# A new order table for a delta-rule attention followed by a SoLU block

## The chip, the cores and the metric

The kernel runs on one core of a Trainium2 chip. A core has five engines that run side by side, each with its own queue of instructions, executed in the order in which they were put there: PE (TensorE, matrix products; its weight loads are counted apart as PEld), DVE (VectorE), ACT (ScalarE), POOL (GpSimd) and SP (SyncE, which here only issues transfers). Transfers (DMA) between the chip's memory and the core's on-chip memory are issued by SP or ACT and run on 16 DMA engines. Products land in PSUM, a small memory of banks, from which DVE and ACT fetch them. The metric is device time in microseconds (us) of one execution; less is better.

## What is computed

```python
# q, k, v: (4, 8, 768, 48) f32; beta: (4, 8, 768)
k_n = k / (norm(k, axis=-1) + 1e-06)
state = zeros((B, H, D, D))
for t in range(S):
    y[:, :, t] = einsum('bhd,bhde->bhe', q[:, :, t], state)
    v_old = einsum('bhde,bhd->bhe', state, k_n[:, :, t])
    state = state + beta_t * einsum('bhd,bhe->bhde', k_n[:, :, t], v_t - v_old)
x = y.transpose(0, 2, 1, 3).reshape(3072, 384)

h = x @ w_in                      # (384, 1024)
sm = softmax(h)                   # with the row's maximum taken off
solu = h * sm
ln = (solu - mean(solu)) / sqrt(var(solu) + 1e-06) * g_ln
out = ln @ w_out                  # (1024, 384)
```

The first part is a recurrence over 768 time steps for 32 pairs of batch and head; the second works on 3072 rows, each by itself. The weights w_in and w_out come as 64-bit numbers.

## The kernel before

**Tiling.** The 768 steps are cut into 12 chunks of 64. Two chunks make a stage, so there are 6 stages (s = 0 to 5). The batches go in two pairs. A *unit* n (0 to 23) is one chunk of one pair of batches with 8 heads each: 128 rows of x. Four units make a stage: n = 4s to 4s + 3. Unit n + 2 continues the state of unit n.

**A stage.** Within a chunk the recurrence becomes a triangular system per head. For each unit `gram_p` (words p and g of the order table) multiplies keys by queries and keys by keys (L444, L447); the first result is masked into `pt` (`p_mask` on DVE, L459, or `p_copy` on ACT with `p_pool` on POOL, L462 and L465), the second is copied by `g_copy` (L471). `g_out` (go, L481) writes it to memory, and `to_inv` (ti, L490) and `to_gx` (tg, L500) read it back in the layout of the inverse. `norms` (no, L512 to L520) makes the keys' norms on DVE. Then `inv_bm`, `inv_ya` (L579, on POOL), `inv_yb` (L586) and `inv` (in, L596 and L600) invert 128 triangular blocks of 32 x 32 a stage, by 30 steps of a product and a sum, each step needing the one before; a word such as `in.4.7.9.1` holds steps 7 and 8 of stage 4, and its last digit chooses POOL (1) or DVE (0). `inv_tz` and `inv_tx` (L606, L613) transpose the result, and the `tlevel` functions (ta, tm, tb, tc; L687 to L711) complete it to 64 x 64. Stage 0 has Gram products of its own (gd, gl), a transpose `gram_dt` (gt), an inverse of blocks of 16 (iv) and levels la, lm, lb, lz, lc, lx above it.

**The state's chain.** For each unit, in turn: `chain_bank` (bk, L730), `chain_r` (r, L736, DVE), `chain_ups` (up, L750), `chain_u` (u, ACT), `chain_kpu` (kp, L774 and L776), `chain_s` (s, L783).

**The MoE part of a unit.** x is split into a high and a low float16 half (y and xl; L788, L792) and transposed by a transfer (xT, L796). `moe_h` (h, L808) makes h in three passes `h.n.0` to `h.n.2` of six products: high by high, high by low, low by high. `sm_max`, `sm_exp`, `sm_pr` (mx, ex, pr), `sm_square` (sq), `sm_z`, `sm_var`, `sm_rr` (z, va, rr), `sm_ln`, `p_hi`, `p_lo` (ln, ph, pl) make the normalized rows, a transfer transposes them (pT, L866), and `moe_o` (o, L873) multiplies by w_out in three passes of eight products. `moe_out` and `store` (ou, st) write out.

**Weights.** `load_w` (W) brings one of 14 blocks: 0 to 5 of w_in (L204), 6 to 13 of w_out (L207). Their 64-bit words are turned into float32 by `w_abs` on ACT and `w_bits` (wb): pieces 0, 1, 2 on DVE (L266, L268, L270) and a last one that is piece 3 on DVE or piece 4 on POOL (L276, L277). Then the high half is made on ACT (wh), the low half on DVE (wl) or on PE and ACT (wu, wc).

**Other loads.** Kn and V bring keys and values of a stage, `L` the key and query block of a unit, LK and LA only its keys (LA by ACT's queue), LQ only its queries; B and G are small.

**Fillers.** fy, fh and fm (`fill`, L188) are products of the identity into a PSUM tile that nobody reads: `fh.7` issues seven.

**The order.** Nothing is scheduled by the compiler: a text, ORDER, holds some 1250 words; each word calls one function with its arguments, and each engine's queue gets its instructions in the order of the words. Waits for data and for buffers follow from the tiles. So a word that stands early holds up whatever stands behind it on the same engine, and SP's transfers also go out in the order of the words. A transfer can be issued by ACT in place of SP where the word ends in 1 (go, ti, tg).

Of the kernel before, what the change touches and what calls it, by code (L numbers as in the profile page):

```python
# [31 lines left out]
V.0.0 W.1 wb.8.1 wb.3.0 wb.10.1 wb.3.1 wl.4 wb.3.2 wb.5.1 lc.1 ta.0 tm.0 lz.1 lc.0 wb.1.0 wb.8.2 lx.0.0 wb.10.2 wa.1
tb.0 tc.0 fv.0.0.1 wb.9.4 wh.9 z1 wb.10.3 wb.1.1 wb.5.2 wb.1.2 wb.1.3 wl.9 p.0 pa.0 pm.0 wb.3.4 wh.3 wh.10 lx.1.1
ti.1.0 up.0 wb.5.4 wb.8.4 gr.1 wh.1 no.1 bm.1 u.0 LQ.1 W.2 wh.5 fh.1 LQ.3 V.1.0 fh.7 ta.1 p.1 kp.0 pa.1 pm.1 wu.5 tm.1
tb.1 wa.2 wc.5 s.0 y.0 la.3 wu.1 W.11 tc.1 wc.1 ya.1 fv.1.0.1 yb.1 in.1.1.3.1 in.1.3.5.1 in.1.5.7.1 in.1.7.9.1
# [1 line left out]
in.1.27.29.1 in.1.29.31.1 wu.3 up.1 lm.3 xl.0 W.0 L.8 LQ.2 lb.3 W.7 xT.0 fy.5 wa.0 wa.11 wb.2.0 wb.2.1 wb.2.2 wl.10
wb.2.3 wb.11.0 wb.0.0 wb.0.1 wb.0.2 wb.0.3 u.1 lz.3 p.8 kp.1 wc.3 wh.2 g.8 wh.0 s.1 pa.8 la.2 h.0.0 wl.2 lm.2 lb.2
wl.0 h.0.1 lc.2 wb.11.1 y.1 pm.8 xl.1 wa.7 lz.2 ta.2 lx.2.1 wh.8 tm.2 W.6 wa.6 h.0.2 tb.2 V.0.1 wb.6.0 wb.6.1 wb.6.2
wb.7.0 wb.7.1 wb.7.2 wb.7.3 wh.7 L.11 L.9 L.10 tc.2 bk.2 gl.0.3 mx.0 wb.11.2 wb.11.3 r.2 ex.0 pr.0 p.10 pa.10 wl.7  # L40
pm.10 up.2 Kn.0.1 xT.1 g.10 V.1.1 p.2 pa.2 wh.11 u.2 sq.0 pm.2 wl.8 wb.6.3 wl.11 W.13 W.12 go.0.2.0 h.1.0 p.9 pa.9
pm.9 kp.2 wh.6 g.9 p.11 h.1.1 h.1.2 wa.13 g.11 y.2 gc.0.3 ta.3 tm.3 lc.3 lx.3.1 tb.3 tc.3 wb.13.0 wb.12.0 wb.12.1 s.2
z.0 xl.2 wb.13.1 wb.12.2 wl.6 mx.1 bk.3 wb.13.2 r.3 va.0 ex.1 wa.12 pr.1 rr.0 wb.13.4 fm.6 up.3 u.3 p.3 pa.3 pm.3 kp.3
sq.1 tz.1 ln.0 pc.11 y.3 zc.1.0 tx.1.0 s.3 xl.3 zc.1.1 tg.1.0 go.1.2.0 fv.0.1.1 z.1.1 pp.11 L.14 xT.2 h.2.0 h.2.1
h.2.2 ta.4 xo.1.0.1 tm.4 mx.2 bk.4 xo.1.1.0 tb.4 r.4 fm.3 ta.5 ex.2 pr.2 ti.2.0 L.13 V.1.2 xT.3 tc.4 tm.5 up.4 ta.6
tb.5 va.1.1 wb.12.4 z.2.1 wh.12 sq.2 fv.1.1.1 fh.7 u.4 tc.5 tm.6 wh.13 ph.0 kp.4 h.3.0 tb.6 ta.7 y.4 h.3.1 tm.7 tc.6
# [922 lines left out]
```

## Time and profile before

| | us |
|---|---|
| median of 3 runs | 414.24 |
| lowest, highest run | 411.41, 414.56 |
| the profiled execution | 411.82 |
| its span, first to last instruction | 410.1 |
| DVE, ACT, POOL busy in it | 285.4, 238.7, 227.6 |

The profile comes from one execution. Its span leaves out 1.7 us at the ends. Busy time is the time in which an engine worked on an instruction; PE's products are pipelined, and the ends that the profile gives them are modelled. The granted clock is what the chip's throttle gave PE, 1.00 being full speed. A wait is put down to the instruction or transfer that ended it; "issue" is time in which an engine waited for nothing that the profile shows.

### The profile page before, as it was taken

Reading aid. Unit: us, or ns where it says so; the run is one execution under the profiler, and the core shown is the slowest. Engines: PE = TensorE matmul, PEld = TensorE weight load, DVE = VectorE, ACT = ScalarE, POOL = GpSimd, SP = SyncE. Lnnn points to the kernel's source line nnn. Section 1 sums busy time; section 2 is a strip of 40 time slices with the busy share of each in tenths; the row PEclk is TensorE's granted clock in tenths of the full one; section 3 lists DMA queues with packets and bytes.
Section 4 is the critical chain, followed back from the end, with each engine's and each line's share of the span. In section 5 each row is a group of like instructions: output and inputs, shape, how many; then the busy total and the mean of one; then the engine's idle time right before and its main releaser. Section 6 shows DMA issues by size and latency. Waiting matters only on the chain.

```text
span 410.1 us, 19489 instructions
## 1 busy us (share of the span) xinstructions
PE 359.0 (88%) x8697; PEld 228.0 (56%) x8697; DVE 285.4 (70%) x539; ACT 238.7 (58%) x486; POOL 227.6 (55%) x393
## 2 busy tenths in 40 slices
...
PEclk9755698968998699959999999999999999999999
...
GB/s 211 270 144 207 247 105 237 154 78 164 110 173 152 72 144 138 233 78 94 175 201 139 164 163 140 176 111 151 104 109 114 107 49 134 84 91 91 121 97 104
DMA packets 114645, 57.82 MB, mean 141 GB/s; under 512 B 102529, under 2 KB 105729, under 8 KB 114561
## 3 DMA queue, kind: packets, MB, share of 16 engines
...
q8 instruction: 68, 1.11, 1.2%
...
q14 instruction: 17, 0.13, 0.1%
...
## 4 chain that ended last, share of the span: by engine, by line
PE 68%; DVE 9%; POOL 7%; issue 6%; DMA 6%; ACT 4%; SPq 1%; POOLq 0%; DVEq 0%; ACTq 0%
PE h L808 22%; PE ops L873 19%; PE bank L730 4%; PE p L444 4%; PE kpu L774 4%; DMA kq<-kq_dram 2%; PE ups L750 2%; PE mps L703 2%; DMA wo<-w_out_dram 2%; PE yps L776 2%; PE mps L687 2%; PE yps L730 1%; PE fill L188 1%; PE g L447 1%; POOL itmp L596 1%
## 5 line engine op out<-in xcount | busy, mean ns | idle before, releaser
L596 POOL TENSOR_TENSOR itmp<-y,ginv 128x30 f32<-128x30 f32 (+14 forms) x116 | 65.3, 563 | 32.8 <-DVE y L600 14.8
L808 PE MATMUL h<-win_hi,xt 128*128 128x512 f16 x288 | 73.7, 392 | 5.5 <-issue 3.1
L873 PEld LDWEIGHTS <-ph 128*128 128x128 f16 x576 | 54.5, 99 | 41.0 <-DMA ph<-pn 4.1
L873 PE MATMUL ops<-wout_hi,ph 128*128 128x384 f16 x384 | 71.1, 331 | 3.3 <-ACT o L877 2.2
L600 POOL TENSOR_TENSOR y<-y,itmp 128x30 f32<-128x30 f32 (+14 forms) x116 | 66.1, 570 | 9.1
L808 PEld LDWEIGHTS <-xt 128*128 128x128 f16 x432 | 40.4, 100 | 53.1 <-issue 12.1
L444 PE MATMUL p<-kq 48*64 48x64 f32 x768 | 34.8, 250 | 9.7 <-DMA wo<-w_out_dram 5.4
L817 DVE TENSOR_REDUCE st<-h 128x1 f32<-128x1024 f32 x24 | 29.2, 1218 | 15.9 <-PE h L808 13.6
L444 PEld LDWEIGHTS p<-kq 48*64 48x64 f32 x768 | 31.1, 162 | 13.5 <-issue 8.1
L808 PE MATMUL h<-win_lo,xt 128*128 128x512 f16 x144 | 37.1, 396 | 0.3 <-issue 0.3
L873 PE MATMUL ops<-wout_lo,ph 128*128 128x384 f16 x192 | 36.5, 335 | 0.0
L828 DVE SCALAR_TENSOR_TENSOR pr<-h,pr 128x1024 f32<-128x1024 f32 x24 | 29.3, 1220 | 9.8 <-ACT pr L823 9.6
L862 DVE TENSOR_TENSOR pn<-pr,pn 128x1024 f16<-128x1024 f32 x24 | 30.5, 1276 | 7.0 <-ACT pn L858 7.0
L855 ACT ACTIVATE pr<-pr,st 128x1024 f32<-128x1024 f32 x24 | 29.8, 1241 | 7.7 <-POOL st L851 7.4
L823 ACT ACTIVATE pr<-h,st 128x1024 f32<-128x1024 f32 x24 | 26.7, 1112 | 12.0 <-DVE st L818 11.8
L850 POOL TENSOR_TENSOR st<-st,nhalf 128x1 f32<-128x1 f32 x24 | 14.0, 583 | 33.6 <-DVE st L846 18.5
L711 ACT COPY zt<-mps 32x128 f32<-32x128 f32 x96 | 24.5, 255 | 11.1 <-PE mps L703 9.8
L730 PE MATMUL yps<-st,kq 48*64 48x48 f32 x704 | 27.0, 226 | 3.6 <-issue 3.6
L836 ACT ACTIVATE pn<-pr,st 128x1024 f32<-128x1024 f32 x24 | 27.5, 1147 | 3.5 <-DVE st L829 3.3
L776 PE MATMUL yps<-u,pt 64*64 64x48 f32 x768 | 28.5, 224 | 1.0 <-DVE pt L459 0.7
L447 PE MATMUL g<-kq 48*64 48x64 f32 x640 | 27.4, 245 | 1.1 <-ACT u L757 1.0
L755 ACT ACTIVATE u<-ups 128x192 f32<-128x192 f32 x24 | 7.9, 329 | 34.5 <-PE upo L750 33.9
...
## 6 DMA issues: line engine op xcount, KB each, us to landing
...
gd<-g SPq DMA_DIRECT2D x8, 512.0 KB, 3.3
...
wi<-w_in_dram SPq DMA_DIRECT2D x6, 512.0 KB, 6.8
...
```

What stands on the lines that cost most here:

```text
L444: nc.tensor.matmul(out=ps[o : o + C, h], lhsT=k[lan, 0, h], rhs=k[lan, 1, h], start=True, stop=True)
L447: nc.tensor.matmul(out=gp[o : o + C, h], lhsT=k[lan, 0, h], rhs=k[lan, 0, h], start=True, stop=True)
L596: eng.tensor_tensor(out=tv, in0=y[:, 0:j, j : j + 1].to_broadcast([P, j, n]), in1=b[:, j : j + 1, j + 1 : 32].to_broadcast([P, j, n]), op= ...
L600: eng.tensor_tensor(out=y[:, 0:j, j + 1 : 32], in0=y[:, 0:j, j + 1 : 32], in1=tv, op=ALU.add)
L730: nc.tensor.matmul(out=ps[o : o + C, h], lhsT=k[lan, i, h], rhs=sb[lan, h], start=i == 0 or h == 0, stop=i == 0)
L776: nc.tensor.matmul(out=yps[n][o : o + C, h], lhsT=p[lan, h], rhs=u[lan, h], start=n < 2, stop=n < 2 or h == H - 1)
L808: nc.tensor.matmul(out=hp[n][:, qs], lhsT=xt[n][:, 3 * a + k], rhs=b[:, k, qs], start=j == 0 and k == 0, stop=j == 2 and k == 2,)
L817: nc.vector.tensor_reduce(out=nmax, in_=hp[n], op=ALU.max, axis=AX.X, negate=True)
L828: nc.vector.scalar_tensor_tensor(out=pr, in0=hp[n], scalar=1.0, in1=pr, op0=ALU.mult, op1=ALU.mult, accum_out=sp)
L855: nc.scalar.activation(pro[n], pro[n], AF.Identity, bias=mean, scale=rr)
L862: nc.vector.tensor_tensor(out=pn[:, 1], in0=pro[n], in1=pn[:, 0], op=ALU.subtract)
L873: nc.tensor.matmul(out=ops_[n], lhsT=pht[n][:, 8 * a + k], rhs=b[:, k], start=j == 0 and k == 0, stop=j == 2 and k == 7)
```

## The change

Only ORDER is replaced; no function is touched. The new table has 1246 words where the old one had 1257. All words of the fillers are gone. Most other words are the same and stand in another order; some change their last digit, so that a step runs on another engine or a transfer goes out by another queue:

- weights: the last piece is done by DVE in place of POOL for blocks 3, 4, 8, 9, 12 and 13, by POOL in place of DVE for blocks 0, 1 and 10; the low half of block 4 is made on PE and ACT, that of block 1 on DVE, each the other way round from before
- masks of units 4, 6 and 11: DVE in place of ACT and POOL
- inverse: 14 words `in` on DVE where there were 17, and others than before; steps 9 and 10 of stage 0 on POOL
- transfers of the Gram blocks: go.1.1 and go.0.3 by SP in place of ACT; tg.1, tg.5 and go.0.4 by ACT in place of SP
- small steps z, va, xo, lx and fv of some units and stages change engines

The diff cut to the first lines, those around the first w_out product and the last ones:

```diff
-Kn.1.0 kx.1.0 kv.1 Kn.0.0 G kx.0.0 kv.0 ca cn fy.13 fh.12 LA.0 LA.1 gd.0.0 gd.0.1 LK.2 gd.0.2 gz.0 z0 cc cb LK.3 B L.4
-fy.6 kr.0 kn.0 kb.0 iz.0 iy.0 gd.0.3 gt.0 ib.0 iv.0.1.3.0 iv.0.3.5.0 iv.0.5.7.0 iv.0.7.9.0 W.8 iv.0.9.11.0 p.4 gg.0
-pc.4 g.4 pp.4 L.5 W.4 W.9 L.7 L.6 W.10 W.3 W.5 p.5 wb.9.0 pc.5 g.5 pp.5 gl.0.0 gl.0.1 p.7 iv.0.11.13.1 iv.0.13.15.1
-pa.7 pm.7 wa.8 g.7 gc.0.0 wa.10 go.1.1.1 p.6 g.6 sg wb.4.0 wb.4.1 wb.4.2 wb.10.0 tz.0 wb.9.1 gl.0.2 pc.6 pp.6 wa.9
...
+W.4 wb.4.0 wb.4.1 Kn.1.0 kx.1.0 kv.1 cc ca iz.0 z1 z0 LA.0 Kn.0.0 LA.1 cn gl.0.0 kx.0.0 kv.0 W.5 wb.5.0 wb.5.1 wb.5.2
+wa.5 kr.0 LK.2 B LK.3 gd.0.0 gd.0.1 gd.0.2 gd.0.3 cb gz.0 wb.5.4 wa.4 gc.0.0 L.5 gl.0.1 p.5 kn.0 kb.0 iy.0 gt.0 W.1 G
+W.10 LQ.0 ib.0 iv.0.1.3.0 iv.0.3.5.0 iv.0.5.7.0 wb.1.0 iv.0.7.9.0 W.0 L.4 L.6 L.7 gl.0.2 gc.0.2 pc.5 g.5 wb.4.2 wb.4.3
+wb.0.0 wb.0.1 pp.5 iv.0.9.11.1 iv.0.11.13.1 iv.0.13.15.1 wh.5 gg.0 wa.10 wa.1 gc.0.1 p.4 pa.4 pm.4 wb.1.1 wb.1.2
+wb.0.2 g.4 wu.5 wh.4 p.7 pa.7 pm.7 V.1.0 W.2 g.7 wa.0 p.6 L.9 W.9 V.0.0 wu.4 tz.0 pa.6 pm.6 tx.0.0 wb.1.4 g.6 la.0
...
+pa.3 pm.3 tz.1 ta.3 lc.3 tm.3 sq.1 go.1.2.0 go.0.2.0 xT.2 W.8 ti.2.0 lx.3.1 tb.3 tc.3 up.3 tx.1.0 u.3 xo.1.0.1 p.13
+kp.3 no.2 pa.13 z.1.1 z.0.1 va.1.1 rr.1 fv.0.1.1 va.0.1 rr.0 fv.1.1.1 zc.1.1 zc.1.0 ln.1 g.13 y.3 xo.1.1.1 wa.8 h.2.0
+ta.4 pm.13 bm.2 ta.7 ya.2 yb.2 in.2.1.3.1 in.2.3.5.1 in.2.5.7.1 in.2.7.9.1 in.2.9.11.1 in.2.11.13.1 in.2.13.15.1
+in.2.15.17.1 xl.3 tm.4 h.2.1 ln.0 s.3 tb.4 tc.4 ph.1 tm.7 V.1.2 Kn.0.1 tg.2.0 L.12 xT.3 Kn.1.1 h.2.2 mx.2 bk.4 ta.5
...
+wb.8.3 wl.7 pl.0 tc.5 up.5 u.5 h.3.2 ta.6 kp.5 wh.8 xT.4 pT.1 V.0.2 L.14 mx.3 wl.8 o.1.0 o.1.1 y.5 tm.6 s.5 xl.5 ex.3
+tc.7 tb.6 bk.6 tc.6 pr.3 in.2.17.19.0 r.6 in.2.19.21.0 in.2.21.23.0 sq.3 z.3.1 va.3.1 rr.3 in.2.23.25.1 in.2.25.27.1
+in.2.27.29.1 in.2.29.31.1 h.4.0 p.12 up.6 h.4.1 pa.12 u.6 g.12 kp.6 pm.12 s.6 ln.3 y.6 ph.3 sq.2 xl.6 h.4.2 p.14 pa.14
...
-ln.21 ph.21 mx.22 ex.22 pr.22 pl.21 z.22 st.16 xT.23 h.23.0 h.23.1 h.23.2 sq.22 ou.18 va.22 rr.22 ln.22 ph.22 pT.19
-o.19.0 o.19.1 o.19.2 mx.23 ex.23 st.18 pT.21 ou.20 pl.22 pr.23 sq.23 z.23.1 va.23.1 rr.23 ln.23 ph.23 pl.23 o.21.0
-o.21.1 o.21.2 st.20 ou.19 pT.22 st.19 o.22.0 o.22.1 o.22.2 ou.21 pT.23 st.21 ou.22 st.22 o.23.0 o.23.1 o.23.2 ou.23
-st.23
+st.17 xT.23 h.23.0 h.23.1 h.23.2 sq.22 va.22.1 rr.22 ou.16 ln.22 mx.23 ph.22 ex.23 o.20.1 o.20.2 pr.23 st.16 pT.21
+o.21.0 o.21.1 o.21.2 pl.22 ou.20 pT.19 o.19.0 o.19.1 o.19.2 sq.23 z.23.1 va.23.1 rr.23 ln.23 ph.23 pl.23 st.20 ou.21
+pT.22 o.22.0 o.22.1 o.22.2 st.21 ou.19 pT.23 st.19 ou.22 st.22 o.23.0 o.23.1 o.23.2 ou.23 st.23
```

The fillers of the old table and the words that followed them: `fy.13 fh.12` and `fy.6` as above, `fh.1` and `fh.7` around LQ.3 before ta.1, `fy.5` before p.8, `fm.6` before up.3, `fm.3` before ta.5, `fh.7` before kp.4, `fm.1` before up.5, `fh.3` before h.6.0.

More of the change, by code (lines that the diff above doesn't have):

```diff
@@ L32 @@
[L32 to L35, printed above, removed]
-in.1.9.11.1 in.1.11.13.1 in.1.13.15.1 in.1.15.17.1 in.1.17.19.1 in.1.19.21.1 in.1.21.23.1 in.1.23.25.1 in.1.25.27.1
@@ L37 @@
[L37 to L46, printed above, removed]
@@ new lines @@
+st.4 up.10 p.19 o.2.1 o.2.2 u.10 g.19 pa.19 mx.8 pm.19 in.3.23.25.0 ex.8 pr.8 kp.10 p.18 h.9.0 h.9.1 in.3.25.27.1
+va.7.1 rr.7 y.10 g.18 ou.2 ln.7 ph.7 xl.10 s.10 in.3.27.29.0 pa.18 pm.18 in.3.29.31.1 go.1.4.0 xT.10 pT.6 go.0.4.1
+st.2 ti.4.0 tz.3 sq.8 zc.3.0 bk.11 h.9.2 o.5.0 p.20 r.11 up.11 pa.20 pl.7 mx.9 u.11 zc.3.1 pm.20 ex.9 tx.3.0 o.5.1
+o.5.2 pr.9 kp.11 ta.12 o.6.0 xo.3.0.1 h.10.0 h.10.1 y.11 sq.9 tm.12 s.11 xl.11 g.20 xo.3.1.1 ou.5 bk.12 ta.13 tb.12
+h.10.2 o.6.1 no.4 fv.0.3.1 fv.1.3.1 z.9.1 va.9.1 rr.9 z.8.1 va.8.1 rr.8 r.12 xT.11 L.21 st.5 pT.7 L.22 ln.9 tm.13
@@ new lines @@
+tc.12 ta.15 up.12 tb.13 ln.8 u.12 mx.10 ex.10 ph.9 tm.15 ph.8 o.6.2 bm.4 ya.4 yb.4 in.4.1.3.1 in.4.3.5.1 pr.10 o.7.0
+kp.12 tb.15 h.11.0 h.11.1 h.11.2 tc.13 y.12 ou.6 in.4.5.7.1 in.4.7.9.1 in.4.9.11.1 z.10.1 s.12 xl.12 pl.9 mx.11 pl.8
+tc.15 ex.11 bk.13 o.7.1 o.7.2 r.13 p.22 up.13 pr.11 tg.4.0 st.6 pT.9 xT.12 ou.7 sq.10 st.7 pT.8 L.23 o.9.0 h.12.0
+pa.22 in.4.11.13.0 pm.22 va.10 sq.11 u.13 in.4.13.15.0 z.11.1 va.11.1 rr.11 rr.10 ta.14 kp.13 g.22 tm.14 tb.14 h.12.1
+h.12.2 ln.11 tc.14 y.13 ln.10 ph.11 p.21 g.21 in.4.15.17.0 s.13 in.4.17.19.1 in.4.19.21.1 in.4.21.23.1 in.4.23.25.1
@@ new lines @@
+in.4.25.27.1 in.4.27.29.1 in.4.29.31.1 xl.13 mx.12 pa.21 pm.21 pl.11 xT.13 go.0.5.0 V.1.4 V.0.4 bk.14 o.9.1 o.9.2 r.14
+p.23 up.14 ex.12 pr.12 h.13.0 h.13.1 h.13.2 ph.10 u.14 ou.9 g.23 pa.23 kp.14 pT.11 o.8.0 o.11.0 o.8.1 o.8.2 o.11.1
+sq.12 y.14 pl.10 pm.23 mx.13 s.14 xl.14 go.1.5.0 ti.5.0 st.9 z.12.1 ex.13 pr.13 z.13.1 fv.0.4.1 xT.14 bk.15 o.11.2
+tz.4 tx.4.0 xo.4.0.0 zc.4.0 ou.8 sq.13 r.15 va.13.1 no.5 bm.5 rr.13 va.12.1 rr.12 h.14.0 zc.4.1 ln.13 up.15 u.15
+xo.4.1.1 ta.18 ta.16 tm.16 h.14.1 h.14.2 ln.12 Kn.0.5 Kn.0.4 st.8 pT.10 kp.15 tb.16 o.10.0 o.10.1 o.10.2 ou.11 y.15
```

81 lines of the change are left out of this document (36 added, 45 removed).

## The prediction

> **What bounds the kernel now.** I read the page's busy shares and slices first, then busy time by stretches, then the chain in order of time, then single stretches of the timeline.
>
> ```profile
> PE 359.0 (88%) x8697; PEld 228.0 (56%) x8697; DVE 285.4 (70%) x539; ACT 238.7 (58%) x486; POOL 227.6 (55%) x393
> PEclk9755698968998699959999999999999999999999
> ```
>
> No engine but PE is near its span, and PE's clock is full from the 19th slice on. The share is an average, so I cut the span where its character changes. The columns are the stretch, its length, then PE, weight loads, DVE, ACT, POOL busy, granted clock, DMA share, GB/s.
>
> ```profile
> 0.00:15.00 15.00, 10.89 (x282) 5.58 (x286) 5.60 (x12) 3.20 (x4) 8.31 (x23) 0.99 0.86 231
> 15.00:60.00 45.00, 29.88 (x1096) 24.30 (x1086) 41.19 (x71) 22.96 (x55) 28.26 (x28) 0.62 0.69 192
> 60.00:100.00 40.00, 30.92 (x1048) 20.86 (x1041) 32.39 (x54) 21.82 (x52) 35.61 (x57) 0.87 0.73 156
> 100.00:145.00 45.00, 38.97 (x1097) 24.84 (x1099) 29.20 (x59) 26.71 (x58) 35.05 (x58) 0.85 0.64 122
> 170.00:190.00 20.00, 15.92 (x436) 10.76 (x429) 9.50 (x19) 9.88 (x23) 9.63 (x17) 0.74 0.52 101
> 190.00:390.00 200.00, 194.69 (x4180) 119.42 (x4178) 142.55 (x278) 133.55 (x260) 97.02 (x182) 1.00 0.68 127
> 390.00:410.00 20.00, 13.53 (x82) 7.57 (x79) 2.88 (x5) 6.45 (x11) 1.45 (x5) 1.00 0.51 103
> ```
>
> There are four regimes. From 15 to 60 DVE is the bound (41.19 of 45 us: weight bits, masks, the first inverse). From 60 to 100 POOL is (35.61 of 40: the inverse of stage 1). From 190 to 390 PE is, at 194.69 of 200 and full clock: an order can win 5.3 us there at the very most. So what an order can change lies in the start, in 100 to 145, in 170 to 190 and in the tail. In 100 to 145 PE idles 6.0 us, and a clock of 0.85 means that 30% of it, 13.5 us, ran at half speed, which loses 6.8 us more: 12.8 in all. In 170 to 190 it idles 4.1 us, and a clock of 0.74 means 10.4 us at half speed, 5.2 lost: 9.3 in all.
>
> Why PE stops at 170 is the most telling place:
>
> ```profile
> 164.03 1.09 SPq L222 DMA_DIRECT2D v<-vn_dram  x1
> 165.18 0.89 SPq L231 DMA_DIRECT2D kq<-kq_dram  x2
> 166.17 0.37 SPq L881 DMA_DIRECT2D out_dram<-o  x1
> 166.58 1.92 SPq L231 DMA_DIRECT2D kq<-kq_dram  x4
> 168.60 1.21 SPq L796 DMA_TRANSPOSE xt<-xn  x1
> 170.22 0.38 PE L687 MATMUL mps<-zt,gx 32*32 32x32 f32 x22
> 172.37 0.23 PE L687 MATMUL mps<-zt,gx 32*32 32x32 f32 x4 [1.77 <-issue]
> 174.33 2.31 issue
> q8 instruction: 68, 1.11, 1.2%
> ```
>
> SP issues nine transfers in 5.8 us. Two us later PE stops in the middle of one group of 32 matmuls, after the 22nd, where no data can be missing: "issue" means that it waited for nothing the profile shows. It does so again for 2.31 us at 174.33. Instructions come as packets of their own (68 of 16 KB), so I read this as PE's program arriving behind a burst of loads; the clock falls after it. By the Trainium skill, Runtime: NRT & Kernel Launch, Instruction fetch mechanics, refills come in 16 KiB blocks and their cost is mostly hidden. The 1.11 MB in 68 packets agrees with the block; the stop in mid-group speaks against "hidden".
>
> **The change part by part.**
>
> *No fillers.* All 64 (actions fy, fh, fm) go.
>
> ```profile
> L188 PE MATMUL fill<-ident 128*128 128x512 f16 x64 | 17.9, 424 | 1.5 <-POOL tiny L155 1.4
> 99.42 2.10 PE fill L188 x6
> 112.33 0.75 PE fill L188 x3
> 115.70 1.62 PE fill L188 x7
> 163.20 0.77 PE fill L188 x3
> 99.52 0.55 DVE L736 TENSOR_TENSOR v<-v,bank 128x384 f32<-128x384 f32 x1 [1.58 <-POOL y L600]
> ```
>
> They take 17.9 us of PE, most of it before 65 us, where PE has room. On the chain they hold 2.10 + 0.75 + 1.62 + 0.77 = 5.24 us. What follows the first of these needs the residual of L736, done at 100.07, so 1.45 of its 2.10 us is true delay. Bounds 0 and -5.2; I take **-3**. The cost of losing them is clock: a rival below.
>
> *The start.* Five weight pieces (wb.4.0, wb.4.1, wb.5.0 to wb.5.2) move ahead of the transpose of the first Gram blocks (gt.0), two w_in loads go ahead of the last key blocks, W.4 ahead of everything.
>
> ```profile
> L266 DVE TENSOR_SCALAR wf<-wi 128x512 int32<-128x512 int32 x6 | 3.2, 528 | 0.0
> L268 DVE SCALAR_TENSOR_TENSOR wf<-wi,wf 128x512 int32<-128x512 int32 x6 | 4.5, 752 | 0.1
> L270 DVE SCALAR_TENSOR_TENSOR wf<-wi,wf 128x512 int32<-128x512 int32 x6 | 5.9, 988 | 0.1
> wi<-w_in_dram SPq DMA_DIRECT2D x6, 512.0 KB, 6.8
> PE p L444 <- DMA wo<-w_out_dram: 5.4, 1, 5.4
> PE dg L392 <- issue: 2.6, 1, 2.6
> 53.73 0.80 DVE L518 TENSOR_TENSOR nb<-nxb,bt 128x32 f32<-128x32 f32 x1
> 54.60 2.31 POOL L579 TENSOR_SCALAR_AFFINE_SELECT y<-nb 128x1024 f32<-128x1024 f32 x1
> ```
>
> The pieces cost 2 x 0.528 + 2 x 0.752 + 0.988 = 3.55 us, and DVE idled 9.4 of the first 15 us, so they are free and DVE is ahead by as much. What counts is when POOL may begin stage 1's inverse: L579 at 54.60, released by DVE's L518. Ahead of it DVE has six w_in pieces more (19 against 13, at the rows' mean of 0.76 us: +4.5), four w_out pieces fewer (6 against 10, three quarters as wide: -2.3), and two masks more against one pair of inverse steps less, which about cancel. That is +2 us of work against 3.55 paid in idle time and an end of the 5.4 us wait below. POOL isn't in the way: five of its seven weight masks (wb.i.4) stood ahead of that point, now four in all do, and the pp masks of units 4 and 6 go to DVE. Against it stand 2 x 512 KB ahead of the keys: at 231 GB/s of the first stretch 4.5 us. They are covered, since gd.0.3 waited 2.6 us for issue and p.5 5.4 us behind bulk weight loads, and L.5 now stands ahead of W.1 and W.10. If that cover fails the start loses up to 4.5; if p.5's whole wait goes it gains 5.4. I take **-3**, the middle of what these leave: 3.55 - 2 = 1.6 if p.5 waits as long as before, 1.6 + 2.7 if half as long.
>
> *Gram by transfer.* go.1.1 and go.0.3 go from ACT's queue to SP, tg.1, tg.5 and go.0.4 from SP to ACT: ACT issues six DMAs before and nine after.
>
> ```profile
> 29.13 0.36 ACTq L481 DMA_DIRECT2D gd<-g  x1
> 81.50 1.49 SPq L500 DMA_DIRECT2D gx<-gd  x2
> ```
>
> Two gx issues took 1.49 us and one gd issue 0.36, so ACT spends 2 x 1.49 + 0.36 = 3.3 us on what comes to it and saves 0.7. Behind them wait ACT's copies; ACT has 200 - 133.55 us free in the long stretch, so 0 is right unless the queue is full: up to +3. On SP both go.1.1 and go.0.1 now stand behind V.1.0, W.2, L.9, W.9 and V.0.0, whose issues fill the time in which SP waited for g.6.
>
> *Stage 2 sooner, w_out products sooner.* tz.1 keeps its neighbours (r.3, pr.1, pm.3 ahead of it). Then no.2 follows at once behind tx.1; before, h.2 and much of unit 4 came first.
>
> ```profile
> 104.59 2.04 DVE L606 STREAM_TRANSPOSE zt<-y 128x1024 f32<-128x1024 f32 x1
> 114.16 0.65 DVE L512 COPY nx<-ginv 128x32 f32<-128x32 f32 x1
> 145.57 1.47 PE L873 MATMUL ops<-wout_hi,ph 128*128 128x384 f16 x8
> ```
>
> That takes about 6 us out of the 9.6 between them. It is worth nothing by itself, as the MoE of units 2 to 7 covers it. But o.1 now stands ahead of bk.6 and h.4, where before the first w_out product ran at 145.57, behind both. PE thus has about 2.7 us more work at hand (two passes of 1.3, the tail's row below) in the very stretch that loses 12.8 us. The fillers' part is counted already; bounds 0 and -12.8; I take a third, **-4**.
>
> *Loads spread.* The burst at 164 was V.1.3, L.16, st.1, L.19, L.17 and xT.7; now L.19 goes at h.5, V.1.3 ahead of h.6, L.16 ahead of h.7 and L.17 behind it. Bounds 0 and -9.3 for 170 to 190; I take half, **-4.5**, since other bursts stay (V.1.2, Kn.0.1, tg.2, L.12, Kn.1.1 in one run).
>
> *Inverse steps.* Of 17 pairs of steps on DVE 14 remain, at other places. That lengthens stage 4's and 5's inverse by a few us, covered by the backlog of MoE work in 190 to 390: 0.
>
> *Tail.* Behind h.23 nine passes of w_out stood; now eleven, two of unit 20 being added.
>
> ```profile
> 378.50 5.20 PE ops L873 x32
> 383.70 3.90 PE h L808 x18
> 402.75 4.09 PE ops L873 x24
> ```
>
> 32 matmuls are four passes, 1.30 each. From the end of h.23 (387.60) to the last product (402.75) are 15.15 us, the softmax chain of unit 23; nine passes fill 11.7 of them, eleven 14.3. So h.23 may end 2.6 sooner; bounds 0 and -2.6; **-2**.
>
> *New stops.* A table laid out against a model meets the chip with other ones. No row shows them. The row nearest is what is lost in one such place, 9.3; the other end is 0; I take **+6.5**, over half.
>
> Sum: -3 - 3 - 4 - 4.5 - 2 + 6.5 = -10. The profiled execution took 411.82 (span 410.1), so 401.8; the median of the runs is 2.4 above it, and I put the new median at **403**, its own range 396 to 410.
>
> **Rivals.** *The stops only move:* the -4 and -4.5 don't come, 403 + 8.5 = 411.5; that is also where it lands if the keys come late (start +4.5 in place of -3, 410.5). For it speaks that bursts remain; against it that the order names their cure. If fetches are hidden, as the skill's Runtime page has it, only the -4.5 fails, and it is 407.5, inside the main case's range.
>
> *The clock (slower):* 60 to 100 ran at 0.87 with fillers. 30.92 busy us hold about 26.9 us of full-speed work; at half speed that is 53.8 in 40, 13.8 too many. With only fillers and tail gained: 411.8 - 3 - 2 + 13.8 = 420.6. It decides if PE's pauses around 60 to 110 us keep the clock at half for more than some 20 us of that stretch. Against it: in 15 to 60 the clock was 0.62 even with fillers, so they didn't hold it. By the Trainium skill, TensorE: Matmul & The Clock Gate, Part 1, the half clock is the default and activity releases it, after about 3.4 us either way; by that rule taking work away can only hurt the clock, and the rows agree as far as the clock falls behind pauses.
>
> *More:* both stretches come back in full and few new stops come: 403 - 13.6 = 389.4, say 392 with some stops.
>
> **Numbers.** Main case 0.45; stops move 0.17, late keys 0.05; clock 0.18; more 0.15. Faster by over 1% (below 410.1; about what a measurement of this kernel can tell from no change): 0.59, the main and the "more" case less a sliver. Within 1%: 0.22. Slower: 0.19, the clock and a sliver. The range 392 to 419 leaves out one in ten at each end.
>
> **What would show it.** Right: L579 of stage 1 starts near 51.6; the first L873 before 135; no PE stop over 1 us in 160 to 200, clock 1.00 there; PE idle behind 385 under 2 us. Wrong: a granted clock below 0.8 in 60 to 100, the first masks (L459) later than before, or new stops "issue" of over 10 us in sum behind 100 us.

## The result and the profile after

| | before | after |
|---|---|---|
| median of the runs, us | 413.62 (411.41 to 414.56, 4 runs) | 397.25 (395.96 to 398.15, 4 runs) |
| the profiled execution, us | 411.82 | 398.15 |
| its span, us | 410.1 | 396.2 |
| mean granted clock in it | 0.917 | 0.940 |

The new order takes 0.961 [0.956, 0.966] of the time of the old one: 16 us less in the medians, 13.7 us less in the two profiled executions, which are compared in what follows. Ratios, here and below, leave out executions in a slower state that any kernel falls into at times, so they need not be the quotients of the medians. No function was touched, so lines stand one lower in the new kernel (L873 is now L872).

The page of the new kernel: busy shares, the granted clock in 40 slices, and the packets that carry PE's program.

```profile
PE 345.4 (87%) x8633; PEld 224.4 (57%) x8633; DVE 278.8 (70%) x521; ACT 238.9 (60%) x487; POOL 221.8 (56%) x404
PEclk9999555899698998999999999999999999999999
q8 instruction: 67, 1.10, 1.2%
```

Busy time by stretches of the new kernel, with the columns of the prediction:

```profile
0.00:15.00 15.00, 5.47 (x268) 4.75 (x272) 9.06 (x12) 5.14 (x8) 11.26 (x25) 1.00 0.91 250
15.00:60.00 45.00, 27.38 (x1007) 22.28 (x1002) 35.99 (x70) 18.44 (x46) 20.73 (x24) 0.76 0.77 212
60.00:100.00 40.00, 33.38 (x1095) 23.59 (x1095) 33.23 (x54) 22.69 (x50) 35.44 (x58) 0.84 0.55 113
100.00:145.00 45.00, 38.80 (x1189) 26.11 (x1189) 37.70 (x71) 30.20 (x68) 32.47 (x60) 0.89 0.72 133
145.00:160.00 15.00, 12.35 (x233) 7.36 (x234) 8.52 (x11) 8.46 (x15) 9.40 (x21) 0.89 0.59 144
170.00:190.00 20.00, 19.20 (x508) 12.12 (x501) 15.49 (x31) 11.59 (x31) 12.43 (x21) 1.00 0.91 161
190.00:376.00 186.00, 183.10 (x4033) 112.74 (x4026) 127.71 (x248) 127.97 (x248) 95.90 (x187) 1.00 0.72 129
376.00:396.00 20.00, 15.76 (x95) 8.92 (x93) 3.75 (x5) 5.81 (x10) 1.46 (x5) 1.00 0.56 128
```

Two stretches of the kernel before, and the second of them in the new one, to which the experiments come back:

```profile
145.00:160.00 15.00, 14.66 (x320) 9.27 (x311) 12.89 (x27) 9.34 (x17) 5.60 (x12) 1.00 0.62 148
160.00:190.00 30.00, 25.49 (x643) 16.12 (x641) 18.67 (x41) 14.66 (x33) 16.27 (x32) 0.83 0.68 143
...
160.00:190.00 30.00, 29.20 (x754) 18.64 (x754) 22.81 (x55) 20.22 (x47) 15.20 (x27) 1.00 0.94 176
```

In 170 to 190 PE now works 19.20 of 20 us at full clock, where it worked 15.92 at 0.74: by the prediction's own rule (idle time, and half of the time at half clock) 0.8 us is lost there in place of 9.3. In the long stretch behind it 2.90 of 186 us are idle, where 5.31 of 200 were. In 100 to 145 it gains little by that rule, 6.20 us idle at 0.89 against 6.03 at 0.85 (11.2 us lost against 12.8); but of PE's busy time before, some 3.9 us were fillers. A loss stands in 145 to 160 that was not there before. In 160 to 190 the DMA engines are busier than before, 0.94 against 0.68, and yet PE hardly stops: it is not that fewer transfers run there. The lines of the timeline that matter for the forecast's steps:

```profile
104.59 0.19 DVE L511 COPY nx<-ginv 128x32 f32<-128x32 f32 x1
130.35 1.47 PE L872 MATMUL ops<-wout_hi,ph 128*128 128x384 f16 x8
147.65 0.25 PE L729 MATMUL yps<-st,kq 48*64 48x48 f32 x1 [3.35 <-issue]
149.63 1.97 DVE L605 STREAM_TRANSPOSE zt<-y 128x1024 f32<-128x1024 f32 x1 [2.19 <-POOL y L599]
380.31 1.47 PE L872 MATMUL ops<-wout_hi,ph 128*128 128x384 f16 x8 [0.59 <-DMA ph<-pn]
388.81 1.47 PE L872 MATMUL ops<-wout_hi,ph 128*128 128x384 f16 x8 [0.53 <-DMA ph<-pn]
```

Stage 2's norms start at 104.59 (114.16 before), its inverse is transposed at 149.63 (162.01 before), the first w_out product runs at 130.35 (145.57 before). One new stop of 3.35 us ends at 147.65. In the tail two waits of 0.59 and 0.53 us stand where there were 2.15 and 1.14. These lines are from the kernel before, the transpose of stage 2's inverse and the two waits of the tail:

```profile
162.01 2.00 DVE L606 STREAM_TRANSPOSE zt<-y 128x1024 f32<-128x1024 f32 x1 [0.26 <-POOL y L600]
397.54 1.47 PE L873 MATMUL ops<-wout_hi,ph 128*128 128x384 f16 x8 [2.15 <-ACT o L877]
402.75 1.47 PE L873 MATMUL ops<-wout_hi,ph 128*128 128x384 f16 x8 [1.14 <-DMA ph<-pn]
```

**Where the time went.** Two orders can't be compared at equal times by what they are doing, so I compare what is left to do. Every matmul but the fillers is counted at the mean time that one of its kind adds to PE's busy time in the kernel before at full clock (matmuls overlap, so this is less than their durations; 321 us in all, the same in every kernel here). The mark at time t is t plus the work that has not ended by then: when the last product would end if nothing more were lost. Its rise from one time to the next is what PE lost between them, to pauses, to the half clock or to fillers (some 4 us of these between 100 and 145). The table has it for all kernels of this study; the experiments are told below.

| kernel | 100 | 145 | 160 | 190 | 300 | last product ends | lost in 160 to 190 |
|---|---|---|---|---|---|---|---|
| before | 374.5 | 390.3 | 390.8 | 400.0 | 403.7 | 406.8 | 9.2 |
| after | 374.2 | 385.8 | 390.0 | 390.3 | 391.3 | 392.9 | 0.3 |
| old, no fillers | 374.5 | 389.7 | 389.9 | 396.1 | 400.0 | 403.8 | 6.2 |
| old, loads spread | 376.4 | 392.5 | 393.2 | 396.5 | 405.2 | 409.0 | 3.3 |
| old, loads spread and early | 374.6 | 390.8 | 391.8 | 399.7 | 404.3 | 407.4 | 7.9 |
| old, then new | 376.6 | 389.1 | 390.6 | 401.1 | 401.5 | 403.1 | 10.5 |
| new, then old | 374.1 | 385.8 | 392.4 | 402.1 | 406.5 | 413.5 | 9.7 |
| old, stage 2 sooner and mixed | 375.6 | 409.2 | 414.9 | 421.9 | 430.2 | 436.3 | 7.0 |
| old, tail alone | 374.6 | 389.2 | 389.6 | 397.6 | 401.7 | 404.8 | 8.0 |
| new, burst back | 374.0 | 385.8 | 385.3 | 391.6 | 391.0 | 392.0 | 6.3 |
| new, not mixed | 373.6 | 385.8 | 387.4 | 391.6 | 390.2 | 392.2 | 4.2 |
| new, o.1 late | 373.9 | 386.6 | 386.2 | 386.5 | 387.5 | 389.4 | 0.3 |
| new, two loads moved | 374.2 | 387.8 | 387.2 | 388.1 | 391.2 | 392.8 | 0.9 |
| new, both of these | 373.7 | 386.9 | 386.5 | 387.4 | 387.5 | 389.5 | 0.9 |

Before to after: even at 100; 4.2 won from 100 to 145 (a rise of 15.8, the fillers' time in it, against 11.6); 3.7 given back from 145 to 160 (0.5 against 4.2), which is the stop at 144 and the half clock behind it; 8.9 won from 160 to 190; 2.7 from 190 to 300 (3.7 against 1.0); 1.5 behind 300. With the 0.3 at 100 that is the whole 13.9. Marks of single executions wander by about 2 us at 100 between kernels with the same words up to there, so only larger differences are read.

### The profile page after: what moved, and what is told of

Its sections match the earlier page's. It is cut to its first block, busy times and chain, and to the rows that moved or that the text cites. A ratio compares the mean times of both kernels' runs of the same rounds, so it can differ in the third digit from the quotient of the medians.

```text
span 396.2 us, 19341 instructions
## 1 busy us (share of the span) xinstructions
PE 345.4 (87%) x8633; PEld 224.4 (57%) x8633; DVE 278.8 (70%) x521; ACT 238.9 (60%) x487; POOL 221.8 (56%) x404
## 4 chain that ended last, share of the span: by engine, by line
PE 42%; POOL 23%; DMA 12%; DVE 11%; issue 8%; SPq 3%; ACT 1%; DVEq 0%; ACTq 0%; POOLq 0%
PE ops L872 15%; PE h L807 12%; POOL y L599 11%; POOL itmp L595 11%; DMA ph<-pn 4%; DMA ginv<-gd 3%; PE p L443 2%; PE bank L729 2%; PE kpu L773 2%; SPq L489 2%; DMA kq<-kq_dram 2%; DMA gd<-g 2%; DVE ginv L572 1%; PE ups L749 1%; DVE y L585 1%
## 5 line engine op out<-in xcount | busy, mean ns | idle before, releaser
L595 POOL TENSOR_TENSOR itmp<-y,ginv 128x84 f32<-128x84 f32 (+14 forms) x122 | 68.4, 560 | 34.6 <-DVE y L599 14.6
L872 PEld LDWEIGHTS <-ph 128*128 128x128 f16 x576 | 54.4, 98 | 39.8 <-DMA ph<-pn 3.7
L599 POOL TENSOR_TENSOR y<-y,itmp 128x84 f32<-128x84 f32 (+14 forms) x122 | 70.4, 577 | 9.6
L872 PE MATMUL ops<-wout_hi,ph 128*128 128x384 f16 x384 | 70.8, 331 | 2.3 <-DMA ph<-pn 2.2
L807 PE MATMUL h<-win_hi,xt 128*128 128x512 f16 x288 | 71.6, 385 | 0.0
L861 DVE TENSOR_TENSOR pn<-pr,pn 128x1024 f16<-128x1024 f32 x24 | 32.0, 1336 | 5.5 <-ACT pn L857 5.5
L872 PE MATMUL ops<-wout_lo,ph 128*128 128x384 f16 x192 | 35.3, 326 | 0.0
L775 PE MATMUL yps<-u,pt 64*64 64x48 f32 x768 | 31.1, 230 | 0.0
L773 PE MATMUL kpu<-u,k 64*64 64x48 f32 x704 | 28.6, 230 | 2.0 <-issue 1.9
L773 PEld LDWEIGHTS kpu<-u,k 64*64 64x64 f32 x704 | 25.3, 145 | 8.6 <-issue 4.4
L775 PEld LDWEIGHTS yps<-u,pt 64*64 64x64 f32 x768 | 27.5, 144 | 2.5 <-issue 1.9
L729 PE MATMUL yps<-st,kq 48*64 48x48 f32 x704 | 25.6, 221 | 3.3 <-issue 3.3
## 6 DMA issues: line engine op xcount, KB each, us to landing
k<-kn_dram SPq DMA_DIRECT2D x12, 392.0 KB, 5.1
```

The costliest lines, as they stand in the source:

```text
L595: eng.tensor_tensor(out=tv, in0=y[:, 0:j, j : j + 1].to_broadcast([P, j, n]), in1=b[:, j : j + 1, j + 1 : 32].to_broadcast([P, j, n]), op= ...
L599: eng.tensor_tensor(out=y[:, 0:j, j + 1 : 32], in0=y[:, 0:j, j + 1 : 32], in1=tv, op=ALU.add)
L729: nc.tensor.matmul(out=ps[o : o + C, h], lhsT=k[lan, i, h], rhs=sb[lan, h], start=i == 0 or h == 0, stop=i == 0)
L773: nc.tensor.matmul(out=kps[lan, h], lhsT=k[lan, z : z + C], rhs=u[lan, h], start=True, stop=True)
L775: nc.tensor.matmul(out=yps[n][o : o + C, h], lhsT=p[lan, h], rhs=u[lan, h], start=n < 2, stop=n < 2 or h == H - 1)
L807: nc.tensor.matmul(out=hp[n][:, qs], lhsT=xt[n][:, 3 * a + k], rhs=b[:, k, qs], start=j == 0 and k == 0, stop=j == 2 and k == 2,)
```

## The experiments

The times of each are medians, its ratio is to the kernel before in runs beside it on the same chip.

**1. The old table without fillers.** All 64 go, nothing else.

```diff
-kv.1 Kn.0.0 G kx.0.0 kv.0 ca cn fy.13 fh.12 LA.0 LA.1 gd.0.0
+kv.1 Kn.0.0 G kx.0.0 kv.0 ca cn LA.0 LA.1 gd.0.0
...
```

> The old table without its 64 fillers, nothing else changed. Theory (the fillers neither cost nor bring much; the gain came from 170 to 190 us): 0 to -3 us against the old kernel, 410.5 to 413.6. Rival 'fillers were a main cost': -5 or more. Rival 'fillers hold the clock': slower by 5 or more, granted clock below 0.8 in 60 to 100 us. If PE's stops are fetches of blocks of 256 instructions, each stop still comes behind an instruction whose number leaves the rest 193 by 256, now at other work, since 128 instructions are gone ahead of 165 us.

Measured 409.36 us, ratio 0.985 [0.966, 1.005]. Its stretches from 15 to 145:

```profile
15.00:60.00 45.00, 27.15 (x999) 23.48 (x991) 39.43 (x69) 20.10 (x48) 27.62 (x27) 1.00 0.70 196
60.00:100.00 40.00, 32.37 (x1082) 22.56 (x1071) 33.79 (x55) 23.80 (x58) 35.69 (x56) 0.83 0.58 148
100.00:145.00 45.00, 37.32 (x1110) 25.52 (x1110) 28.96 (x57) 28.28 (x61) 32.43 (x55) 0.77 0.65 129
```

Without fillers the clock in 15 to 60 was 1.00 where it had been 0.62, and in 60 to 100 it was 0.83 where it had been 0.87. So the fillers did not hold the clock up in the start, and the forecast's slower rival, which needed the half clock in most of 60 to 100, did not come. In 100 to 145 it may be otherwise: the clock was 0.77, and 0.85 to 1.00 in the five kernels of this study that have the old words up to there with the fillers in them. What the fillers cost is not settled: the interval reaches from -14 to +2 us. From 100 to 145 the place of the fillers is taken by other losses: PE idles 7.68 us there at a clock of 0.77, 18.0 us lost by the rule of the prediction against 12.8, and the mark at 160 is only 0.9 better than before. In 160 to 190 it loses 6.2 in place of 9.2, with one stop of 2.81 us where there were two.

**2. The old table with the burst at 164 spread.** L.16 goes behind the transpose xT.8, V.1.3 and L.19 behind Kn.1.3.

```diff
-y.8 pT.2 pT.3 V.1.3 L.16 st.1 tb.10
+y.8 pT.2 pT.3 st.1 tb.10
...
-o.3.2 L.19 L.17 xT.7 st.0 xT.8 L.18
+o.3.2 L.17 xT.7 st.0 xT.8 L.16 L.18
...
-pm.16 Kn.1.3 xT.9
+pm.16 Kn.1.3 V.1.3 L.19 xT.9
```

> The old table with five loads moved out of the burst at 164 to 170 us: L.16 behind xT.8, V.1.3 and L.19 behind Kn.1.3. Theory (a burst of loads delays PE's instructions, then the clock falls): -5 to -9 us, 404.5 to 408.5, no PE stop over 0.6 us in 165 to 180 and clock 1.00 in 170 to 190. Rival (the stops have another cause, or come back elsewhere): within 2 us of the old kernel.

Measured 414.93 us, ratio 1.002 [0.996, 1.008]. The stretches 160 to 190 and 190 to 300, and what PE met next:

```profile
160.00:190.00 30.00, 27.61 (x710) 17.50 (x702) 23.71 (x53) 19.41 (x42) 20.18 (x39) 1.00 0.70 115
190.00:300.00 110.00, 102.34 (x2484) 63.85 (x2482) 83.53 (x169) 68.86 (x136) 65.67 (x122) 0.98 0.86 156
199.12 0.27 PE L444 MATMUL p<-kq 48*64 48x64 f32 x1 [1.79 <-DMA kq<-kq_dram]
```

The cure works in its place, though not wholly: 2.39 us idle at full clock in 160 to 190, 5.9 us less lost than in the kernel before, but a stop of 1.49 us is still there at 175, where none of over 0.6 was expected. Then p.19 waits for the very load L.19 that was put off, the clock is no longer full (0.98 over the 110 us), and from 190 to 300 the marks rise by 5.0 us more than before. Spreading alone wins nothing.

**3. The same, with the loads put off less.** L.16 behind xT.8, L.19 behind L.18, V.1.3 behind Kn.1.3.

```diff
-o.3.2 L.19 L.17 xT.7 st.0 xT.8 L.18
+o.3.2 L.17 xT.7 st.0 xT.8 L.16 L.18 L.19
...
-pm.16 Kn.1.3 xT.9
+pm.16 Kn.1.3 V.1.3 xT.9
```

> The old table with L.16 behind xT.8, L.19 right behind L.18 and V.1.3 behind Kn.1.3: as in e2_spread, but L.19 early enough for p.19. Theory (e2_spread won 5.5 us in 170 to 190 and lost 4 around 197 where p.19 waited for L.19): -4 to -6 us, ratio 0.985 to 0.991. Rival (what is won there is lost again behind it, whatever the place of the loads): ratio 0.996 to 1.006.

Measured 412.46 us, ratio 1.001 [0.996, 1.005]. Here 7.9 us are lost in 160 to 190 though SP issues only a store, L.17 and a transpose at 165 to 168, four transfers for nine. PE still stops for 1.77, 1.09 and 0.96 us, the first two at the same places of its program as in the kernel before. So the burst is not all of it.

**4. Splices.** The old words up to tz.2 and then the new order of what is left, and the other way round.

```diff
 y.7 s.7 pl.3 pr.5 xl.7 ou.1
-tz.2 bk.8 fv.0.2.1 fh.3 tx.2.0 r.8
+L.19 Kn.1.3 tz.2 z.4.1 fv.1.2.1 fv.0.2.1 tx.2.0 va.4 rr.4
...
```

> The old table up to the word ahead of tz.2 (162 us in the old profile), fillers included; from there all words that are left, in the order of the new table. Theory (the gain lies behind 160 us): -9 to -13 us, 400.5 to 404.5. Rival (it lies in the first 150 us: fillers, start, earlier w_out products): no more than -4, 409.5 or above.

> The new table up to the word ahead of tz.2 (149 us in the new profile); from there all words that are left, in the order of the old table. Theory (gain behind 160 us): between -5 and +2 us against the old kernel, 408.5 to 415.5, less where its burst of loads is thinner by the two that the new part has already sent. Rival (gain in the first 150 us): -8 us or more, 405.5 or less.

Old then new: 408.85 us, ratio 0.992 [0.987, 0.998]. New then old: 418.80 us, 1.019 [1.005, 1.032]. Neither half carries the gain. In the first, PE's timeline has these at the seam:

```profile
164.74 0.45 PE L687 MATMUL mps<-zt,gx 32*32 32x32 f32 x32 [2.71 <-DVE zt L606]
168.90 2.74 PE L873 MATMUL ops<-wout_hi,ph 128*128 128x384 f16 x8 [3.70 <-DMA ph<-pn]
```

The new order has the level products of unit 8 ahead of h.6 and w_out passes right behind them. With stage 2's inverse as late as in the old kernel the first have to wait for it. The second wait is not its doing: o.3 waits for its transposed rows, whose transfer SP issued at 163.52, behind the store st.1, which had waited 4.1 us for ACT. The half clock stands from 166.19 to 173.02, and 10.5 us are lost. From 190 on the new order loses 2.0 us up to the end, the old one 6.8 in the kernel before. The second splice came out slower than was expected of it (up to 415.5). By the marks it loses 6.6 us in 145 to 160, the stop at 144 among them, 9.7 in 160 to 190 and 7.0 behind 300, where the kernel before loses 0.5, 9.2 and 3.1; why the last of these grew stays open.

**5. The new table with the burst back.** L.19, L.16 and L.17 right behind V.1.3.

```diff
-ta.8 xT.6 V.1.3 Kn.0.2 o.0.1
+ta.8 xT.6 V.1.3 L.19 L.16 L.17 Kn.0.2 o.0.1
```

> The new table with a burst put back: L.19, L.16 and L.17 issued right behind xT.6 and V.1.3 (161 to 163 us in the new profile), ahead of stage 2's run of small products. Theory (a burst of loads holds up PE's fetches there): the ratio to the old kernel rises from 0.961 to 0.97 to 0.983, 4 to 9 us, with PE stops 'issue' between 163 and 185 us of over 2 us in sum. Rival (the new order has enough large products there to hide fetches whatever is loaded): ratio 0.957 to 0.966.

Measured 400.81 us, ratio 0.973 [0.966, 0.980], where the new table has 0.961 [0.956, 0.966].

```profile
169.98 0.57 PE L773 MATMUL kpu<-u,k 64*64 64x48 f32 x2 [1.54 <-DMA k<-kn_dram]
175.52 2.74 PE L872 MATMUL ops<-wout_hi,ph 128*128 128x384 f16 x8 [3.20 <-DMA ph<-pn]
```

The burst costs 6.3 us in 160 to 190 again, but not as the forecast had it: no stop "issue" comes (none of over 0.3 us between 144 and 273), PE waits for data that landed behind the burst, keys first and transposed rows then. In the total less is seen of it: with L.19 gone from its old place the stop at 144 is 1.32 us, and the mark at 160 is 4.7 better than the new table's.

**6. The new table with its small products in one run.** Four large passes go behind ta.11, so that the chain and level products of units 8 to 11 follow each other, as they did in the old table; the loads stay.

```diff
-in.3.9.11.1 h.6.0 o.3.2 ta.9 tb.10 up.8 h.6.1 h.6.2 xT.7
+in.3.9.11.1 ta.9 tb.10 up.8 xT.7
...
-tb.9 ta.11 o.4.0
+tb.9 ta.11 h.6.0 o.3.2 h.6.1 h.6.2 o.4.0
```

> The new table with four large passes (h.6.0, o.3.2, h.6.1, h.6.2) moved behind ta.11, so that bk.8, ta.10, tb.8, ta.9, tb.10, up.8, kp.8, tb.9 and ta.11 stand in one run, as in the old table; loads stay where they are. If small products without large ones between them bring the stops: stops or waits of 2 us and more in sum between 165 and 176 and a half clock behind them, 3 to 6 us slower than the new table, 400 to 403. If only the loads count: 397 within 1.

Measured 399.29 us, ratio 0.968 [0.959, 0.977]: 2 us above the new table, within what the two intervals allow to be nothing. In the stretch itself the loss is there:

```profile
160.00:190.00 30.00, 28.08 (x693) 18.15 (x692) 20.23 (x50) 17.46 (x43) 13.47 (x26) 0.89 0.82 167
165.06 0.42 PE L686 MATMUL mps<-zt,gx 32*32 32x32 f32 x28 [1.38 <-ACT zt L710]
167.14 0.34 PE L773 MATMUL kpu<-u,k 64*64 64x48 f32 x1 [0.41 <-ACT u L754]
```

1.92 us idle and a clock of 0.89 in place of 0.80 idle and 1.00, 4.2 us lost by the marks in place of 0.3: with no large pass between, small products wait for ACT's copies of those before them, and the half clock stands from 166.18 to 173.01, behind the first wait. No stop for the program fell into the stretch, so that part of the expectation did not come.

**7. The old table with stage 2 sooner and its small products mixed.** The first thirteen words of stage 2's inverse move ahead to h.2, the others to r.6, and o.1 and o.0.2 go among the level products.

```diff
-xT.2 h.2.0 h.2.1 h.2.2 ta.4
+xT.2 ti.2.0 h.2.0 h.2.1 h.2.2 no.2 bm.2 ya.2 yb.2 in.2.1.3.1 in.2.3.5.1 in.2.5.7.1 in.2.7.9.1 in.2.9.11.1
+in.2.11.13.1 in.2.13.15.1 in.2.15.17.1 in.2.17.19.1 ta.4
...
-pl.1 h.4.0 h.4.1 bk.6 h.4.2 pT.0 L.15 xT.5 r.6 up.6
+pl.1 h.4.0 h.4.1 bk.6 h.4.2 pT.0 L.15 xT.5 r.6 in.2.19.21.0 in.2.21.23.0 in.2.23.25.0 in.2.25.27.1 in.2.27.29.1
+in.2.29.31.1 up.6
...
+mx.5 o.1.0 kp.7 ex.5 ta.9 ta.8 tm.8 o.0.2 tb.8 tc.8 tm.9 ta.10 y.7 s.7 o.1.1 tm.10 tb.9 pl.3 pr.5 xl.7 bk.8 o.1.2
...
```

> The old table with stage 2's inverse started some 6 us sooner (no.2 to in.2.15 right behind h.2, the later steps behind r.6, tz.2 and tx.2 ahead of mx.5) and the small products of units 8 to 10 (ta, tb, up.8) mixed with the passes o.1 and o.0.2 in place of standing in one run behind h.6. Theory that it is the run of small products without large ones between them that outruns the arrival of the program: no stop "issue" of over 1 us between 160 and 185, no half clock there, 4 to 7 us faster, 407 to 410. Should the large products now be missing later (a wait of o.3 for its transposed rows), the gain shrinks to 2. Theory that only the burst of loads counts: the two stops of 1.8 and 2.3 us stay near 170 to 177, as the burst does, and the time is 413 within 1.

Measured 438.35 us, ratio 1.055 [1.045, 1.066]: a miss, and a telling one (the execution profiled took 441.29). ACT's and PE's timeline:

```profile
145.51 0.61 ACT L281 ACTIVATE wout_hi<-wf,g_sb 128x384 f16<-128x384 f32 x1 [19.40 <-POOL wf L277]
147.52 0.34 PE L774 MATMUL kpu<-u,k 64*64 64x48 f32 x1 [16.70 <-ACT u L755]
```

The inverse took POOL for itself; wb.12.4, a piece of w_out's bits, stood behind it; wh.12 on ACT waited 19.40 us for that piece; u.4, behind wh.12 on ACT, held PE's kp.4 for 16.70 us. So stage 2's inverse can't simply be put sooner in the old table. In the new one the last piece of block 12 is done by DVE, a hundred words ahead of the inverse, and POOL does no other piece behind it. Whether mixing alone cures the old order this run can't say, since its stretch starts from another state.

**8. The new table with the first w_out passes late.** o.1.0 and o.1.1 go behind h.4.2.

```diff
-mx.3 wl.8 o.1.0 o.1.1 y.5 tm.6
+mx.3 wl.8 y.5 tm.6
...
-xl.6 h.4.2 p.14
+xl.6 h.4.2 o.1.0 o.1.1 p.14
```

> The new table with the first two passes o.1.0 and o.1.1 moved back behind h.4.2. Prediction's term (w_out products sooner fill PE where it idles): 4 us slower, ratio 0.968 to 0.973. Theory after the result (they bring PE work forward, and the stop at 144 takes it away again): within 1.5 us, ratio 0.957 to 0.966.

Measured 395.29 us, ratio 0.960 [0.953, 0.967], no slower. Putting w_out's first products ahead of bk.6 and h.4 is worth nothing that the runs can tell. The stop at 144 is gone too.

**9. The new table with two loads moved,** L.19 ahead of L.18 and Kn.1.3 behind V.0.3.

```diff
-xT.5 L.15 pT.0 L.19 Kn.1.3 go.0.3.0
+xT.5 L.15 pT.0 go.0.3.0
...
```

> The new table with L.19 moved from 139 us to ahead of L.18 (186 us) and Kn.1.3 from 141 us to behind V.0.3 (195 us). Theory: the stop of 3.35 us at 144.30 and the half clock of 3.4 us behind it came from the loads at 139 to 141; without them the stop is under 1 us: -3 to -5 us, ratio 0.949 to 0.954. Rival (L.15, pT.0 and go.0.3 alone hold up the fetch): stop stays over 2.5 us, ratio 0.957 to 0.966.

Measured 396.48 us, ratio 0.958 [0.949, 0.966]. The stop at 144 is gone, a wait of 1.96 us for DVE's residual at 136.6 has come; the mark at 160 is 387.2 in place of 390.0.

**10. Both of these at once.**

```diff
-mx.3 wl.8 o.1.0 o.1.1 y.5 tm.6
+mx.3 wl.8 y.5 tm.6
...
-xT.5 L.15 pT.0 L.19 Kn.1.3 go.0.3.0
+xT.5 L.15 pT.0 go.0.3.0
...
```

> The new table with both small edits tried before: o.1.0 and o.1.1 behind h.4.2, L.19 ahead of L.18 and Kn.1.3 behind V.0.3. Each alone took away the stop of 3.35 us at 144 and came out 1 to 2 us below the new table in the runs. Both cure the same stop, so they don't add up: 394 to 396, ratio 0.955. If what they won was only the place of a fetch, a third place brings a stop back: 397 to 398.

Measured 395.67 us, ratio 0.962 [0.956, 0.969]. Its marks from 160 on are 3 to 4 us below the new table's, but its ratio isn't. None of the three edits can be told from the new table by the runs.

**11. The tail alone, in the old table.** o.20.1 and o.20.2 go behind h.23.2.

```diff
-pT.20 o.20.0 o.20.1 o.20.2 pl.19
+pT.20 o.20.0 pl.19
...
-h.23.0 h.23.1 h.23.2 sq.22
+h.23.0 h.23.1 h.23.2 o.20.1 o.20.2 sq.22
```

> The old table with the passes o.20.1 and o.20.2 behind h.23.2, as in the new one. If the tail term is right: PE's waits behind h.23 fall from 3.3 to 1 us or less, 2 us faster, ratio 0.995. If the softmax chain of unit 23 grows by what the passes hold up: no difference.

Measured 411.85 us, ratio 0.995 [0.990, 1.000].

```profile
380.78 1.45 PE L808 MATMUL h<-win_hi,xt 128*128 128x512 f16 x6 [1.56 <-DVE pr L828]
391.78 1.48 PE L873 MATMUL ops<-wout_hi,ph 128*128 128x384 f16 x8 [0.46 <-DMA ph<-pn]
396.80 1.47 PE L873 MATMUL ops<-wout_hi,ph 128*128 128x384 f16 x8 [0.94 <-DMA ph<-pn]
```

The waits behind h.23 fall from 3.29 to 1.40 us, by as much as forecast though not to 1, but h.23 itself, with less ahead of it, now has a wait of 1.56 us that DVE's softmax step (pr, L828) ends, and the marks rise by 3.1 from 300 to the end as they did before. The ratio, 2 us, is at the edge of what it can tell from nothing.

## Why the prediction was right, point by point

The median came out at 397.25 where 403 was forecast, inside its range and on its side. The sum was -10 and the profiled executions differ by 13.7. (Carried over to the median the sum gives 401.8 + 2.4 = 404.2; 403 was put a little below it.) The total holds better than its terms:

- **Fillers, -3.** Not shown. Without them the old table gains between 14 and -2 us, and its mark at 145 is 0.6 better. The statement behind it, that the clock does not hang on them, holds in the start (1.00 against 0.62); in 100 to 145 the clock was lower without them (0.77).
- **Start, -3.** Wrong in sign at the place named: L578 of stage 1 (L579 in the prediction) begins at 55.90, not near 51.6 as forecast, and 1.3 later than before. What the forecast counted on did come: p.5 ends at 21.00 in place of 24.59, its long wait behind weight loads gone. But it priced no stops for PE's program in the start. The new kernel's chain of waits, from 39 to 56, and POOL's timeline:

```profile
39.49 3.49 issue
...
46.49 4.62 issue
51.11 0.28 PE xt L667 x4
...
52.00 0.14 ACT zt L710
...
53.67 0.25 ACT nn L344
...
55.02 0.36 DVE nxb L514
```

```profile
55.90 1.27 POOL L578 TENSOR_SCALAR_AFFINE_SELECT y<-nb 128x1024 f32<-128x1024 f32 x1 [9.91 <-DVE nb L517]
```

  Two stops of 3.49 and 4.62 us hold stage 0's products; ACT's norm of stage 1 stands behind copies of those products, DVE's norms behind ACT, and POOL behind DVE for 9.91 us. At 100 us both kernels are even.
- **Stage 2 sooner, 0.** It came 12.4 us sooner (149.63 against 162.01), twice what was forecast, and by itself it may be worth nothing; but "covered" was the wrong reading. The splice that has the new order without the early inverse loses 10.5 us in 160 to 190; 2.71 of them are a wait for stage 2, with the half clock behind it, while 3.70 are the wait for rows whose transfer stood behind a store. So the new order of that stretch needs the inverse early, and how much of the 10.5 that is worth is not measured. Run 7 shows that in the old table it has a price on POOL and ACT.
- **w_out products sooner, -4.** The stretch 100 to 145 did win 4.2, but not for the reason given: with o.1 back behind h.4.2 the kernel is as fast. Some 3.9 is just the time of the fillers that stood there; but run 1, which takes out these alone, wins 0.6. All kernels with the new words up to there stand at 385.8 to 387.8 at 145, all with the old ones but run 7 at 389.1 to 392.5. Which of the new words keep other losses out of their place stays open.
- **Loads spread, -4.5.** The right place, and twice the forecast: 8.9 by the marks, 8.5 by the stretches, close to the bound of 9.3. The mechanism is half right. That loads hold up PE's program is borne out at 144 (last section). But in 170 to 190 the old order stops at the same places with far fewer loads issued (run 3), and the new order does not stop with the burst back: 6.3 are lost again then, but through late data. What the new order has there is 26 large products in the block of the program that ends at the first of these places, where the old one has 6, so PE takes 6.9 us for that block and not 3.5 (last section). With the small products unmixed 4.2 are lost with the loads as they are; and spreading the loads in the old order moves the loss behind 190. The step that fell short was to take the burst for the one cause. The runs point to three conditions: loads apart yet in time, stage 2 early, and large passes between the small products. That they must hold all at once is not shown: no run brings all three into the old table, and for unmixing the loss is seen in the stretch alone, as the ratio of run 6 does not tell it from nothing.
- **Tail, -2.** 3.29 us of waits became 1.12, and by the marks 1.5 less was lost behind 300. The edit alone, in the old table, took the waits away too, but let h.23 wait in their place; there it is not told from nothing.
- **New stops, +6.5.** The one at 144 with the half clock behind it cost 4.2 (from 385.8 to 390.0 in the marks), and those of the start are told above. Behind 100 us the stops "issue" are fewer than before: 1.28, 3.35, 1.05 and 0.56 us, 6.2 in sum, against eleven of 10.9 in sum; in the whole span they are 25.1 us in 14 stops, against 21.5 in 18. So 6.5 was not a number that the runs confirm at any one place.
- **Not forecast:** 2.7 us between 190 and 300, where the stops shrink from 3.3 to 1.6 us in sum and two waits for ACT's copies of level products (0.51 and 1.25) are gone. The prediction had named 5.3 as the most to be won in the long stretch, and then gave it no term.

Of the signs that were set beforehand, the first w_out product (130.35), PE's stops in 160 to 200 (none of over 1 us, clock 1.00) and the idle time behind 385 (0.53 us) came as said; the start of L579 did not.

So the answer was right because the place where the profile showed PE idle most, 170 to 190, paid almost in full, because the tail paid most of its term, and because a stop that was expected somewhere came. That the sum came so near is in part luck: terms worth -3, -3 and -4 rested on reasons that the runs do not bear out, the largest one was half of what came, and 2.7 us were won where nothing had been put down.
